# A plan of scheduler settings per stretch of 32 units, and a calibrated exponential, in a kernel of attention and gMLP layers

## Chip, cores, metric

One NeuronCore of a Trainium2 chip. The metric is the device time of one execution in microseconds (us). The runs came from several chips, so kernels are compared only through the runs of the kernel before that were made on the same chip in the same call, or directly when they shared a call.

## The reference

Two layers, each a multi-query attention (2048 tokens, 32 heads of 16, one shared key and value head) and a gMLP mixer whose spatial gate is a 2048 x 2048 matmul.

```python
q = (x @ wq).reshape(B, S, H, Dh).transpose(0, 2, 1, 3);  k = x @ wk;  v = x @ wv
p = softmax(einsum("bhqd,bkd->bhqk", q, k) * Dh ** -0.5)
x = x + einsum("bhqk,bkd->bhqd", p, v).transpose(0, 2, 1, 3).reshape(B, S, H * Dh) @ wo
z = gelu(layernorm(x) @ w_in);  z1, z2 = z[..., :Fh], layernorm(z[..., Fh:])
g = einsum("ts,bsf->btf", w_sp, z2) + b_sp[None, :, None]        # the spatial pass
x = x + (z1 * g) @ w_out
# ... all of this twice
```

## The kernel before

The program is built by a small list scheduler in the kernel file: operations with a modelled duration are committed in modelled time, and each engine's list is written in that order, with waits on semaphores. The model's times do not exist on the chip; only the order does. A unit is one key tile of one group of heads, four blocks of 512 score columns; there are 1024 units, 512 a layer. A block's exponential is done on ScalarE (1536 or 1024 columns in one instruction) or on VectorE (six instructions, three blocks at a time). What VectorE takes is decided here:

```python
def d_act(n):                       # modelled duration of an exponential on ScalarE
    return n * 0.8333e-3 + 0.051
...
def take(self, t, js):              # may VectorE have a block now? (cut)
    if self.hold or sc.bank_free() > t or sc.free["dve"] > t + JIT:
        return None
    if EF and any(o.start is None and o.ready is not None and o.ready <= t for o in k.early_first):
        return None                 # yield to the spatial pass
    ...
        backlog = sc.free["dve"] - t + sum(o.dur for o in sc.ready["dve"] if o.eng == "dve" and o.ready <= t)
        if backlog > BACKLOG:       # 3.0
            return None
    ...
    u = max(self.u, fu + LOOK)      # LOOK = 8 units ahead of the score matmuls
```

Zero matmuls fill TensorE where the scheduler believes that it would be too idle to keep its clock (with zeros of half the width, e7, the granted clock of a profile was 0.906, with the full ones on the same chip, e5, 0.994):

```python
class WarmStream:
    def peek(self, f): ...          # the time at which the modelled activity of a 3.41 us window falls too low
    def commit(self, t):
        def fn(e):
            return e.matmul(k.b32(pvb if b is None else b.idx), k.zero[:], k.zero[:, None, :].to_broadcast([P, 4, P]),
                            start=b is not None, stop=b is not None)
```

The softmax here doesn't subtract the row's maximum and nothing guards it: scores larger than these inputs give would overflow.

## Time and profile before

| | before |
|---|---|
| time | 1796.68 us median of 4 runs (1796.06 to 1797.44) |
| ScalarE busy | 1724.7 of 1797.9 us (the profile is of a fifth run, of 1799.73 us) |
| exponentials on ScalarE, blocks on VectorE | 1428 instructions, 532 blocks |
| last exponential of layer 0, of layer 1 | 851.2, 1743.8 us |
| from the last exponential to the end | 54.1 us |

The lines that carry this are in the prediction. One more view matters later: the exponentials' own groups, with busy time and mean of one, then the idle time before them and what ended it. Neighbouring instructions overlap: the durations of all exponentials sum to 2085.3 us, where ScalarE was busy for 1724.7 with everything.

```profile
L1471 ACT ACTIVATE Pa<-ps_all 128x1536 bf16<-128x1536 f32 x708 | 1184.4, 1673 | 13.3 <-PE ps_all L1815 9.8 <-PE ps_all L1558 3.2
L1471 ACT ACTIVATE Pa<-ps_all 128x1024 bf16<-128x1024 f32 x720 | 892.7, 1251 | 1.5 <-PE ps_all L1815 1.4
```

L1815 are the score matmuls. L1558 is PV, which waits for VectorE's blocks too and frees ScalarE's ring of results: 3.2 us of ScalarE's idle time come from VectorE being late (in the two places VectorE's block was done at 442.53 and 672.94 us, and PV followed at 443.09 and 673.20). Other lines met below: L1196 are the matmuls of the spatial pass, L1037 the projection of the last tokens into the mixer, L1253 the piece of the spatial pass that needs those last tokens. What runs after the last exponential I call the closing.

### The profile page before, as it was taken

To read this page: it belongs to the slowest core of one execution; us is meant where nothing else is said; L and a number is where in the kernel's file an instruction comes from. 1 tells how busy PE (TensorE), PEld (TensorE's weight loads), DVE (VectorE), ACT (ScalarE), POOL (GpSimd) and SP (SyncE) were. 2 spreads that over 40 slices of the span, in tenths; PEclk is the share of its full clock that TensorE was granted. 3 is DMA by queue.
4 is the path that set the end of the run, shared out by engine and by line. 5 is a ranking of instruction groups with operands and counts; after the bars stand their busy time and mean duration, and the time that the engine had idled before them with its cause. 6 is when DMAs were issued, how large, how long until landed. Compare 5 with 4: busy or idle time off the path is not lost.

```text
span 1797.9 us, 29587 instructions
## 1 busy us (share of the span) xinstructions
PE 1577.4 (88%) x11812; PEld 467.1 (26%) x11812; DVE 1643.8 (91%) x2477; ACT 1724.7 (96%) x1558; POOL 54.1 (3%) x99
## 2 busy tenths in 40 slices
PE   8888888888889898999998888888888999988999
PEld 4222222222222222223532222222222222222235
DVE  8999999999999999883999999999999899999638
ACT  8999999999999999999589999999999999999984
POOL 1000000000000000000110000000000000000000
PEclk9999999999999999999999999999999899999999
DMA  4535100011011020111310000100111001111114
GB/s 148 123 78 134 54 18 4 7 30 24 10 47 31 27 48 4 63 38 53 82 41 10 4 7 19 19 7 4 31 30 39 28 19 48 19 28 40 52 57 122
DMA packets 146761, 74.04 MB, mean 41 GB/s; under 512 B 99776, under 2 KB 143424, under 8 KB 146624
## 3 DMA queue, kind: packets, MB, share of 16 engines
q1 hardware_dynamic: 145040, 71.98, 15.4%
q8 instruction: 94, 1.54, 0.4%
q14 instruction: 43, 0.35, 0.1%
q10 hardware_dynamic: 1584, 0.16, 0.1%
HBM read 31.49 MB, written 17.83 MB: 27 GB/s over the span
## 4 chain that ended last, share of the span: by engine, by line
ACT 55%; issue 21%; PE 19%; DVE 5%; POOL 0%; DMA 0%; ACTq 0%; POOLq 0%
ACT Pa L1471 52%; PE ps_all L1815 5%; PE ps_all L1196 4%; PE ps_all L1558 3%; PE ps_all L1286 2%; PE ps_all L1796 1%; PE ps_all L1253 1%; PE ps_all L998 1%; DVE st L660 1%; ACT z2n L1083 1%; ACT z1s L1079 1%; PE ps_all L1037 1%; DVE xn L675 0%; PE ps_all L966 0%; DVE E L1667 0%
## 5 line engine op out<-in xcount | busy, mean ns | idle before, releaser
L1471 ACT ACTIVATE Pa<-ps_all 128x1024 bf16<-128x1024 f32 (+1 forms) x1428 | 1615.8, 1460 | 14.8 <-PE ps_all L1815 11.1
L1815 PE MATMUL ps_all<-qs,kT 32*128 32x512 bf16 x4096 | 564.4, 386 | 197.0 <-ACT Pa L1471 183.9
L1667 DVE TENSOR_SCALAR E<-ps_all 128x512 f32<-128x512 f32 x532 | 359.6, 681 | 24.2 <-PE ps_all L1815 21.3
L1815 PEld LDWEIGHTS ps_all<-qs,kT 32*128 32x128 bf16 x4096 | 139.3, 91 | 793.2 <-ACT Pa L1471 770.1
L1796 PE MATMUL ps_all<-zero 128*128 128x512 bf16 x1040 | 322.6, 393 | 16.5 <-DVE mv L1126 5.0
L1558 PE MATMUL ps_all<-Pa,V 128*32 128x512 bf16 x3564 | 317.4, 386 | 0.3 <-DVE Pd L1698 0.2
L1698 DVE SCALAR_TENSOR_TENSOR Pd<-E 128x1536 uint16<-128x1536 f32 (+1 forms) x178 | 310.3, 1743 | 2.1
L1558 PE MATMUL ps_all<-Pd,V 128*32 128x512 bf16 x532 | 179.6, 386 | 0.0
L1196 PE MATMUL ps_all<-wsT,z2n 128*128 128x512 bf16 x616 | 170.1, 385 | 0.9 <-DVE gp L1208 0.5
L1696 DVE TENSOR_TENSOR E<-E 128x1536 f16<-128x1536 f16 (+1 forms) x178 | 168.6, 947 | 2.3
L1694 DVE TENSOR_TENSOR E<-E 128x1536 f16<-128x1536 f16 (+1 forms) x178 | 168.4, 946 | 2.4
L1692 DVE TENSOR_SCALAR E<-E 128x1536 f16<-128x1536 uint16 (+1 forms) x178 | 168.9, 949 | 1.8
L1796 PEld LDWEIGHTS ps_all<-zero 128*128 128x128 bf16 x1040 | 79.2, 98 | 183.1 <-issue 125.0
L1695 DVE TENSOR_SCALAR E<-E 128x1536 f16<-128x1536 f16 (+1 forms) x178 | 97.5, 548 | 1.1
L1558 PEld LDWEIGHTS ps_all<-Pa,V 128*32 128x32 bf16 x3564 | 61.9, 94 | 114.4 <-issue 106.0
L1208 DVE TENSOR_TENSOR gp<-ps_all,gp 128x512 f16<-128x512 f32 x56 | 38.4, 686 | 57.7 <-PE ps_all L1196 57.7
L998 PE MATMUL ps_all<-w_in_r,xnTB 128*128 128x448 bf16 x256 | 64.6, 356 | 1.1 <-DVE E L1667 0.4
L1196 PEld LDWEIGHTS ps_all<-wsT,z2n 128*128 128x128 bf16 x616 | 44.8, 98 | 75.3 <-issue 42.6
L1037 PE MATMUL ps_all<-xnTB,w_in_r 128*128 128x512 bf16 (+2 forms) x364 | 63.0, 299 | 1.0 <-DVE z2n L1009 0.3
L1286 PE MATMUL ps_all<-E 128*128 128x512 bf16 x224 | 54.5, 380 | 0.1
L664 POOL TENSOR_SCALAR ve<-mv 128x2 f32<-128x2 f32 (+1 forms) x28 | 12.4, 444 | 1396.6 <-DVE mv L662 1396.4
L1265 ACT ACTIVATE E<-ps_all 128x512 f16<-128x512 f32 (+1 forms) x51 | 26.0, 539 | 25.6 <-PE ps_all L1253 25.0
(86 smaller groups left out, 961.2 us busy)
## 6 DMA issues: line engine op xcount, KB each, us to landing
wsT_scratch<-gp SPq DMA_DIRECT2D x16, 512.0 KB, 3.5
wsT<-wsT_scratch SPq DMA_DIRECT2D x8, 1024.0 KB, 5.4
z1s<-z_scratch SPq DMA_DIRECT2D x16, 448.0 KB, 3.8
z_scratch<-z1s SPq DMA_DIRECT2D x4, 896.0 KB, 5.8
z2n<-wsT_scratch SPq DMA_DIRECT2D x4, 768.0 KB, 4.6
wsT<-wsT_scratch SPq DMA_DIRECT2D x4, 768.0 KB, 5.8
X<-in_A_x_dram SPq DMA_DIRECT2D x8, 256.0 KB, 5.6
z2n<-wsT_scratch SPq DMA_DIRECT2D x2, 1024.0 KB, 8.4
```

The lines of the kernel that those rows point to most:

```text
L1196: ins = e.matmul(self.b32(b), self.z2n[:, s, f * 128:(f + 1) * 128], w_[:, s - s0, :] if s - s0 < na or not spare else wsp[:, s - s0 - na, :],
L1286: ins = e.matmul(self.b32(b)[:, 0:D], self.hT[:, par, f, tt * 128:(tt + 1) * 128], self.w_out_r[:, f, :], start=(f == 0), stop=(f == NF - 1))
L1471: return e.activation(k.Pa[:, base:base + n, :], k.b32(b0, n).rearrange("p (k q) -> p k q", k=n), ACTF.Exp, scale=SCALE)
L1558: ins = e.matmul(k.b32(u.grp.pvb)[32 * j:32 * j + 32, :], k.V[:, u.kt, :], b.slot, tile_position=(0, 32 * j), start=u.first, stop=u.last)
L1667: c = k.sc.op("dve", lambda e: e.tensor_scalar(k.ey[:, s, 512 * i:512 * (i + 1)], k.b32(j.bank.idx)[:, 0:512], E_LOG2, E_BIAS, op0=ALU.mul ...
L1692: o2 = sc.op("dve", lambda e: e.tensor_scalar(x, lo, E_X * 2.0 ** -16, E_X * E_A, op0=ALU.mult, op1=ALU.add), d_sb(n, 0.521e-3), self.ops ...
L1694: o3 = sc.op("dve", lambda e: e.tensor_tensor(w, x, x, ALU.mult), d_sb(n, 0.521e-3), [o2, self.wfree], pr)
L1695: o4 = sc.op("dve", lambda e: e.tensor_scalar(w, w, E_C, None, op0=ALU.add), d_sb(n, 0.26e-3), [o3], pr)
L1696: o5 = sc.op("dve", lambda e: e.tensor_tensor(w, w, x, ALU.mult), d_sb(n, 0.521e-3), [o4], pr)
L1698: o7 = sc.op("dve", lambda e: e.scalar_tensor_tensor(po.bitcast(U16), y, E_D, w, op0=ALU.add, op1=ALU.add), d_sb(n, 1.042e-3), [o5] + self ...
L1796: return e.matmul(k.b32(pvb if b is None else b.idx), k.zero[:], k.zero[:, None, :].to_broadcast([P, 4, P]), start=b is not None, stop=b i ...
L1815: return e.matmul(self.b32(bank), self.kT[32 * j:32 * j + 32, g.v, kt * 128:(kt + 1) * 128], self.qs[32 * j:32 * j + 32, g.q.slot, :], til ...
```

## The change

The intent: let VectorE take blocks as suits each stretch instead of by one setting, and give the scheduler the exponential's average pace on the chip.

```diff
-EF = 1
-LOOK = 8
-BACKLOG = 3.0
+PACE = 0.0125
+STRETCH = 32
+WAYS = ((8, 3.0, 1), (7, 3.0, 1), (9, 3.0, 1), (8, 2.2, 1), (8, 4.2, 1), (8, 3.0, 0), (7, 4.2, 1), (9, 2.2, 1))
+PLAN = (1, 0, 0, 0, 2, 1, 0, 0, 0, 1, 2, 1, 2, 1, 1, 0, 1, 0, 2, 2, 1, 0, 1, 0, 2, 5, 0, 5, 2, 0, 5, 0, 0)
 ...
-        o = k.sc.op("act", fn, d_act(512 * n), self.deps, 0.0, table="exp")
+        o = k.sc.op("act", fn, d_act(512 * n) + PACE, self.deps, 0.0, table="exp")
 ...
-        if EF and any(o.start is None and o.ready is not None and o.ready <= t for o in k.early_first):
+        look, back, ef = WAYS[PLAN[k.fill_s.u // STRETCH]]
+        if ef and any(o.start is None and o.ready is not None and o.ready <= t for o in k.early_first):
 ...
-            if backlog > BACKLOG:
+            if backlog > back:
 ...
-        u = max(self.u, fu + LOOK)
+        u = max(self.u, fu + look)
```

The plan uses only ways 0, 1, 2 and 5: look-ahead of 8, 7 or 9, and not yielding.

## The prediction

> **What bounds the kernel now.** I read the page first for the busiest engine, then the chain that ended last, then each engine's busy time by 50 us windows, then ScalarE's timeline for its gaps, last TensorE's timeline at the end.

> Busy time and chain, from the page:

> ```profile
> PE 1577.4 (88%) x11812; PEld 467.1 (26%) x11812; DVE 1643.8 (91%) x2477; ACT 1724.7 (96%) x1558; POOL 54.1 (3%) x99
> ACT 55%; issue 21%; PE 19%; DVE 5%; POOL 0%; DMA 0%; ACTq 0%; POOLq 0%
> ```

> Three engines are near full; ScalarE (ACT), which takes most of the softmax exponentials, leads. The windows give us, then busy (and count) of PE, PEld, DVE, ACT, POOL, clock, DMA share, GB/s:

> ```profile
> 350.00:400.00 50.00, 41.02 (x318) 10.26 (x317) 49.37 (x64) 50.00 (x46) 0.00 (x0) 1.00 0.10 27
> 800.00:850.00 50.00, 49.65 (x360) 15.07 (x359) 16.33 (x29) 49.88 (x46) 0.81 (x2) 1.00 0.16 51
> 1250.00:1300.00 50.00, 40.74 (x320) 10.03 (x317) 48.46 (x62) 50.00 (x45) 0.00 (x0) 1.00 0.10 27
> 1700.00:1750.00 50.00, 49.66 (x352) 15.72 (x350) 18.29 (x32) 47.69 (x44) 0.81 (x2) 1.00 0.13 40
> 1750.00:1800.00 50.00, 46.40 (x293) 26.48 (x291) 39.37 (x99) 18.34 (x34) 1.10 (x2) 1.00 0.42 121
> ```

> Two kinds of stretch. In the long attention stretches ACT is full and VectorE (DVE) has 0.6 to 1.5 us idle in 50. At the end of each layer (800 to 850, 1700 to 1750) the spatial pass of the mixer fills PE; ACT is still almost full, and DVE has over 30 us idle. After 1743.8 us no exponentials are left and a closing of 54 us runs on PE.

> ACT's timeline: start, length, line, shapes, count, then idle before and its releaser:

> ```profile
> 418.99 23.19 ACT L1471 ACTIVATE Pa<-ps_all 128x1536 bf16<-128x1536 f32 x20
> 443.54 44.39 ACT L1471 ACTIVATE Pa<-ps_all 128x1536 bf16<-128x1536 f32 x39 [1.36 <-PE ps_all L1558]
> 599.42 72.43 ACT L1471 ACTIVATE Pa<-ps_all 128x1536 bf16<-128x1536 f32 x64 [0.31 <-PE ps_all L1815]
> 673.65 94.11 ACT L1471 ACTIVATE Pa<-ps_all 128x1536 bf16<-128x1536 f32 x83 [1.79 <-PE ps_all L1558]
> ```

> The exponentials alternate 1536 and 1024 columns; 64 of them in 72.43 us is 2.263 us a pair. The two gaps before 443.54 and 673.65 are waits for PV (L1558), which frees ACT's ring of results: DVE's exponentials came late there. ACT's other idle time inside the exponentials is 3.1 us from 1397 to 1404 us, 0.8 at 1672, and a few us spread over the start of layer 1. So before the closing, the time is very nearly the sum of ACT's work.

> [...]the trace has 2.263, a fixed 0.065 us each. I use the trace.
> [...]the trace's rows of the chain have 549, 949 to 952 and 1749.
> [...]Sixteen L1196 in a row took 3.46 us here (1748.87 to 1752.33), 216 ns each.
> [...]

> **The change part by part.** All orders are decided when the program is built, so I compared the two built programs' instructions, by count and place, without any time from the scheduler.

> 1. The added 0.0125 us is only in the scheduler's duration of an exponential. Its old pair was 2560 x 0.8333 ns + 2 x 51 ns = 2.235 us; the new one is 2.260, which is the trace's pitch to 0.003. Nothing runs slower by it. Believing ACT slower, the scheduler fits in more DVE blocks per ACT instruction.
> 2. The plan sets look-ahead (7, 8, 9 units), tolerated DVE backlog (2.2, 3.0, 4.2 us) and, in three stretches of layer 1, lets DVE blocks go although spatial work is waiting. Stretches 25, 27 and 30 have this last setting.
> 3. Result in the built program: blocks of 512 columns on DVE go from 532 to 545, so ACT has 13 fewer. By PV order: units 0 to 415, 234 to 235; 416 to 511, 34 to 37; 512 to 799, 160 to 163; 800 to 927, 70 to 69; 928 to 1023, 34 to 41. Seven of thirteen are in the last 96 units.

> Cost on DVE, from these groups (busy us, mean ns):

> ```profile
> L1667 DVE TENSOR_SCALAR E<-ps_all 128x512 f32<-128x512 f32 x532 | 359.6, 681 | 24.2 <-PE ps_all L1815 21.3
> L1698 DVE SCALAR_TENSOR_TENSOR Pd<-E 128x1536 uint16<-128x1536 f32 x177 | 309.6, 1749 | 2.1
> L1692 DVE TENSOR_SCALAR E<-E 128x1536 f16<-128x1536 uint16 x177 | 168.5, 952 | 1.8
> L1696 DVE TENSOR_TENSOR E<-E 128x1536 f16<-128x1536 f16 x177 | 168.2, 950 | 2.3
> L1694 DVE TENSOR_TENSOR E<-E 128x1536 f16<-128x1536 f16 x177 | 168.0, 949 | 2.3
> L1695 DVE TENSOR_SCALAR E<-E 128x1536 f16<-128x1536 f16 x177 | 97.2, 549 | 1.0
> ```

> 359.6/532 is 0.676; the five chain rows sum to 911.5 us over 531 blocks, 1.717. A block costs DVE 2.39 us; 13 cost 31.1. DVE should be busy about 1675 us. Most of it lies beside other work, in the idle time at the layers' ends.

> Saving on ACT, layer 0: 712 exponentials become 711, with 2048 columns fewer: 2048 x 0.833 ns + 0.065 = 1.8 us. Layer 1: 716 become 712, 4608 columns fewer: 3.84 + 4 x 0.065 = 4.1 us. Together 5.9 us, all in stretches where ACT is full.

> What is given back: PE is full in the last stretch, and faster exponentials do not shrink the spatial pass. In the built program 54 instead of 44 spatial matmuls (L1196) stand after the last score matmul, and 44 instead of 36 after the last PV. PE's timeline there, before:

> ```profile
> 1754.94 1.73 PE L1037 MATMUL ps_all<-xnTB,w_in_r 128*128 128x128 bf16 x28
> 1756.51 1.03 PE L1196 MATMUL ps_all<-wsT,z2n 128*128 128x512 bf16 x4
> 1758.01 3.01 PE L1253 MATMUL ps_all<-z2n 128*128 128x256 bf16 x26 [0.48 <-DVE z2n L1134]
> ```

> In the changed order these 4 are 12. Twelve take 12 x 0.216 = 2.6 us from 1756.51, to 1759.1 instead of 1758.01: 1.1 us later, as 0.5 us of the wait absorbs some. Between last scores and last PV, ten L1196 stand where eight did: about 0.4 us. Sum 1.5 us. At the end of layer 0 the order after the last PV is unchanged (46 on both sides), so its 1.8 us is kept. Small copies swap engines (three V copies more on ACT in layer 1, one key copy and one query copy fewer); I put that at zero. The 35 extra zero matmuls (1040 to 1075) cost 35 x 0.216 = 7.6 us of PE in stretches where it has 8 or more us of 50 idle: zero.

> Sum: -1.8 - 4.1 + 1.5 = -4.4 us, to 1792.3. I take off 0.8 for gaps that a scheduler with the right pace should lose (6.3 us are there in the three places named), a guess of about an eighth: 1791.5.

> **The rivals.** DVE becomes the bound: in windows of 350 to 400 us it has 0.6 us idle, less than one block, and a block without room costs 2.39 us to save 0.43. If the six blocks outside the last stretch found no room, that is 6 x 2 = 12 us worse than the sum: about 1804. Against: three of those six fall in layer 0's last 96 units, where DVE idles; the other movements are +1, +3 and -1. More probable is a single new gap of 1 to 3 us at a PV: 1793 to 1795.
> The spatial pass eats all of it: the last seven blocks' gain (3.0 us of ACT) is wholly given back on PE instead of half. For: PE is 49.66 of 50 busy there. That makes 1793.
> The correct pace helps more than counts show: if the 6.3 us of gaps all go, 1786. Against: those gaps hang on where a few late DVE chains fall, which the new plan moves rather than removes.

> **Range and chances.** The countable part is -4.4 us; unknown is where gaps of 1 to 2 us open and close, with some five places known today. Two or three such gaps either way give 1786.5 to 1797. To leave 2% would take 36 us, more than DVE's whole extra work: 1% for faster, 1.5% for slower.

> **What would show it.** Right: 1428 exponentials become 1423, 13 more L1667, DVE near 1675 us; the last exponential of layer 0 ends near 849.3 (851.2 before) and that of layer 1 near 1737 to 1738 (1743.8); from there to the end 55.6 us instead of 54.1. Wrong: new ACT gaps released by L1558 or L1815 in the long stretches (DVE was the bound), a closing no longer than 54.1 us (the spilled spatial matmuls were free), or ACT's gaps below 2 us in all (pace was worth more).

The sum: -1.8 - 4.1 + 1.5 - 0.8 = -5.2 us, from 1796.68 to 1791.5. Its terms rest on the kernel's own trace. The 0.833 ns a column: from the start of one exponential to that of the next, 1330 ns is the most frequent time after 1536 columns (294 of 689) and 903 ns after 1024 (227 of 716), 427 ns for 512 columns or 0.834 each. The 0.065 us: of 2.263 us a pair, 2560 columns leave 0.13 us for two. The 0.216 us: sixteen L1196 in 3.46 us. That the two gaps are VectorE's lateness is in the trace too (442.53 and 672.94 us, above).

## More of the kernel before

Which blocks go to VectorE, and where all work stands in the engines' lists, I call a program's composition.

## The result and the profile after

| | before | after |
|---|---|---|
| time, median | 1796.68 us (4 runs) | 1790.62 us (4 runs, 1789.19 to 1795.45) |
| ratio | | 0.9971 (95% interval 0.9952 to 0.999) |
| exponentials on ScalarE, blocks on VectorE | 1428, 532 | 1423, 545 |
| last exponential of layer 0, of layer 1 | 851.2, 1743.8 us | 847.9, 1738.6 us |
| from the last exponential to the end | 54.1 us | 55.1 us |

A ratio is the mean time of one kernel's fast runs over that of the other's of the same rounds, so it is not quite the ratio of the medians. The profiled run of after is its slowest (1795.45); a later profile of the same program, in e9, has 845.8 and 1735.7 us for the two ends, and again 55.1 from there.

The page of after, busy time and chain:

```profile
PE 1583.5 (88%) x11847; PEld 468.2 (26%) x11847; DVE 1666.6 (93%) x2510; ACT 1719.4 (96%) x1553; POOL 54.2 (3%) x99
ACT 45%; PE 19%; DVE 18%; issue 17%; DMA 0%; POOL 0%; ACTq 0%; POOLq 0%
```

ScalarE's work is 5.3 us less. VectorE's six groups are 32 us more (13 blocks of 2.39 us are 31), though its own busy time rises by only 22.8 us; neighbouring VectorE instructions overlap, 154.9 us in sum before and 170.4 after, and the groups count the overlap twice. VectorE has gone from 5% to 18% of the chain. That is not the 13 blocks' doing alone: e1, with the old 532 blocks, has 17% already.

The exponentials' groups after (the kernel's lines moved down by one or two):

```profile
L1472 ACT ACTIVATE Pa<-ps_all 128x1536 bf16<-128x1536 f32 x706 | 1170.9, 1659 | 12.9 <-PE ps_all L1817 12.0
L1472 ACT ACTIVATE Pa<-ps_all 128x1024 bf16<-128x1024 f32 x716 | 880.9, 1238 | 1.5 <-PE ps_all L1817 1.2
```

The waits for PV (now L1559) are gone altogether; the waits for score matmuls (now L1817) are somewhat more. ScalarE's timeline shows which are left in layer 0 between 100 and 700 us:

```profile
121.48 316.50 ACT L1472 ACTIVATE Pa<-ps_all 128x1536 bf16<-128x1536 f32 x280 [0.77 <-PE ps_all L1817]
438.60 51.72 ACT L1472 ACTIVATE Pa<-ps_all 128x1536 bf16<-128x1536 f32 x45 [0.61 <-PE ps_all L1817]
586.33 177.91 ACT L1472 ACTIVATE Pa<-ps_all 128x1536 bf16<-128x1536 f32 x157 [0.42 <-PE ps_all L1817]
```

The kernel before had breaks of 1.36, 0.31 and 1.79 us in this part, at 443, 599 and 673 us; the longest run without a break is not longer now (280 exponentials, before 364, from 30.56 to 442.18 us). The first of the three breaks has a cause that I had not looked for. Windows of 3.41 us around it, with TensorE's busy time first and its granted clock (PEclk) behind the engines:

```profile
108.41:111.82 3.41, 2.87 (x24) 0.81 (x24) 3.38 (x8) 3.41 (x5) 0.00 (x0) 1.00 0.00 0
111.82:115.23 3.41, 2.99 (x21) 0.73 (x19) 3.34 (x4) 3.41 (x4) 0.00 (x0) 1.00 0.00 0
115.23:118.64 3.41, 2.28 (x23) 0.61 (x22) 3.41 (x6) 3.41 (x5) 0.00 (x0) 0.99 0.00 0
118.65:122.06 3.41, 3.41 (x18) 0.68 (x15) 3.38 (x5) 2.64 (x3) 0.00 (x0) 0.51 0.94 62
```

A count that weighs a matmul by the part of the array that it uses does. Take each matmul's columns in the window (at 216 ns for 512), times the share of the 128 x 128 array: a quarter for the score matmuls (32*128) and PV (128*32), one for a zero matmul. The windows from 108.41 and 111.82 us have 4405 and 4939 columns, that from 115.23 has 2976. In all profiles with such a window, 6677 windows at full clock: all 53 under 2945 columns were followed by half the clock, none of the 6570 above 3141, and in between 19 were and 35 were not, which the count does not explain. In the two profiles of before and after alone, the nine that were followed by it have 2258 to 3036 columns, and all others at full clock between 10 and 1785 us 3072 or more. The scheduler's own limit in the kernel file is 3060.

In the half-clock window the score matmuls came late and ScalarE idled 0.77 us.

The kernel before has such windows too, and one of the prediction's three places of gaps, 1397 to 1404 us, lies in and just behind three of them in a row:

```profile
1392.34:1402.58 10.24, 9.71 (x41) 1.85 (x41) 8.57 (x13) 7.38 (x7) 0.00 (x0) 0.50 0.24 72
1668.82:1672.23 3.41, 3.41 (x19) 0.58 (x16) 3.38 (x6) 2.97 (x3) 0.43 (x1) 0.50 0.40 125
```

So 3.1 of the 6.3 us, and the 0.8 at 1672, were half-clock windows, which neither pace nor plan was meant to change.

Each run's granted clock, recorded for all runs but the first four of the kernel before, tells how many such windows it had: (1 - clock) x span / (0.5 x 3.413 us). A clock of 0.993 is 7 of them, 0.999 one. Within a kernel and chip this goes with 84% of the variance of the time: the four runs of after had 7, 2, 1 and 2 windows at 1795.45, 1790.45, 1789.19 and 1790.79 us. Over all kernels but the one with thin zero matmuls (e7), the slope of time on windows within a kernel and chip is 0.85 us a window (a correlation; e7 tests the cause). With it each kernel has a time at zero windows, which is steadier than the median: for after 1788.8, 1788.8 and 1788.7 us on three chips, for before 1793.7, 1794.6 and 1794.4.

TensorE at the end, after:

```profile
1749.58 1.73 PE L1038 MATMUL ps_all<-xnTB,w_in_r 128*128 128x128 bf16 x28
1751.15 2.75 PE L1197 MATMUL ps_all<-wsT,z2n 128*128 128x512 bf16 x12
1753.74 3.00 PE L1254 MATMUL ps_all<-z2n 128*128 128x256 bf16 x26
```

Twelve spatial matmuls (L1197, in the kernel before L1196) take 1751.15 to 1753.74, 2.59 us, and L1254 follows at once without the old wait of 0.48. From L1038's start to L1254's start it is 4.16 us; in the kernel before it was 3.07. That is the 1.1 us that was expected.

### The profile page after: what moved, and what is told of

It is laid out like the page before. It is cut to its first block, busy times and chain, and to the rows that moved or that the text cites. A ratio compares the mean times of both kernels' runs of the same rounds, so it can differ in the third digit from the quotient of the medians.

```text
span 1793.7 us, 29695 instructions
## 1 busy us (share of the span) xinstructions
PE 1583.5 (88%) x11847; PEld 468.2 (26%) x11847; DVE 1666.6 (93%) x2510; ACT 1719.4 (96%) x1553; POOL 54.2 (3%) x99
## 4 chain that ended last, share of the span: by engine, by line
ACT 45%; PE 19%; DVE 18%; issue 17%; DMA 0%; POOL 0%; ACTq 0%
ACT Pa L1472 44%; PE ps_all L1817 5%; PE ps_all L1197 4%; DVE E L1669 3%; PE ps_all L1559 3%; DVE Pd L1700 3%; PE ps_all L1287 2%; DVE E L1694 2%; DVE E L1696 1%; DVE E L1698 1%; PE ps_all L1798 1%; DVE st L661 1%; PE ps_all L1038 1%; PE ps_all L999 1%; DVE z2n L1010 1%
## 5 line engine op out<-in xcount | busy, mean ns | idle before, releaser
L1472 ACT ACTIVATE Pa<-ps_all 128x1536 bf16<-128x1536 f32 (+1 forms) x1423 | 1611.0, 1446 | 14.4 <-PE ps_all L1817 13.2
L1817 PE MATMUL ps_all<-qs,kT 32*128 32x512 bf16 x4096 | 565.6, 387 | 177.9 <-ACT Pa L1472 159.7
L1669 DVE TENSOR_SCALAR E<-ps_all 128x512 f32<-128x512 f32 x545 | 368.2, 684 | 15.2 <-PE ps_all L1817 13.9
L1798 PE MATMUL ps_all<-zero 128*128 128x512 bf16 x1075 | 331.6, 392 | 19.4 <-DVE mv L1127 7.5
L1817 PEld LDWEIGHTS ps_all<-qs,kT 32*128 32x128 bf16 x4096 | 139.6, 91 | 770.6 <-ACT Pa L1472 743.2
L1700 DVE SCALAR_TENSOR_TENSOR Pd<-E 128x1536 uint16<-128x1536 f32 x182 | 318.0, 1747 | 2.3
L1559 PE MATMUL ps_all<-Pa,V 128*32 128x512 bf16 x3551 | 317.6, 387 | 0.2
L1559 PE MATMUL ps_all<-Pd,V 128*32 128x512 bf16 x545 | 182.9, 386 | 0.1
L1698 DVE TENSOR_TENSOR E<-E 128x1536 f16<-128x1536 f16 x182 | 173.0, 950 | 2.3
L1696 DVE TENSOR_TENSOR E<-E 128x1536 f16<-128x1536 f16 x182 | 173.1, 951 | 2.1
L1694 DVE TENSOR_SCALAR E<-E 128x1536 f16<-128x1536 uint16 x182 | 173.0, 950 | 1.3
L1197 PE MATMUL ps_all<-wsT,z2n 128*128 128x512 bf16 x616 | 167.7, 382 | 3.0 <-DVE gp L1209 1.5
L1697 DVE TENSOR_SCALAR E<-E 128x1536 f16<-128x1536 f16 x182 | 100.3, 551 | 1.2
L1559 PEld LDWEIGHTS ps_all<-Pa,V 128*32 128x32 bf16 x3551 | 61.7, 94 | 114.2 <-issue 106.8
L1038 PE MATMUL ps_all<-xnTB,w_in_r 128*128 128x512 bf16 (+2 forms) x364 | 63.5, 299 | 3.6 <-DVE E L1669 2.6
L1197 PEld LDWEIGHTS ps_all<-wsT,z2n 128*128 128x128 bf16 x616 | 45.0, 98 | 78.2 <-issue 37.8
L665 POOL TENSOR_SCALAR ve<-mv 128x2 f32<-128x2 f32 (+1 forms) x28 | 11.5, 412 | 1398.5 <-DVE mv L663 1398.4
```

The source lines that it names most:

```text
L1197: ins = e.matmul(self.b32(b), self.z2n[:, s, f * 128:(f + 1) * 128], w_[:, s - s0, :] if s - s0 < na or not spare else wsp[:, s - s0 - na, :],
L1472: return e.activation(k.Pa[:, base:base + n, :], k.b32(b0, n).rearrange("p (k q) -> p k q", k=n), ACTF.Exp, scale=SCALE)
L1559: ins = e.matmul(k.b32(u.grp.pvb)[32 * j:32 * j + 32, :], k.V[:, u.kt, :], b.slot, tile_position=(0, 32 * j), start=u.first, stop=u.last)
L1669: c = k.sc.op("dve", lambda e: e.tensor_scalar(k.ey[:, s, 512 * i:512 * (i + 1)], k.b32(j.bank.idx)[:, 0:512], E_LOG2, E_BIAS, op0=ALU.mul ...
L1694: o2 = sc.op("dve", lambda e: e.tensor_scalar(x, lo, E_X * 2.0 ** -16, E_X * E_A, op0=ALU.mult, op1=ALU.add), d_sb(n, 0.521e-3), self.ops ...
L1696: o3 = sc.op("dve", lambda e: e.tensor_tensor(w, x, x, ALU.mult), d_sb(n, 0.521e-3), [o2, self.wfree], pr)
```

## The experiments

For the theories I use a measure taken from each trace: for two neighbouring exponentials, the time from start to start minus 0.8333 ns a column (0.834 by the most frequent times, see the prediction) and 63.5 ns, summed. It is what the exponentials lose to waiting, late ones less the catching up. The 63.5 ns are an average: in the kernel before 718 of 1405 neighbouring pairs have 49 to 53 ns and 590 have 59 to 70. I split it into what falls into (or up to 4 us behind) half-clock windows and the rest, "lost outside".

The theories at the start. A, my prediction's ledger: the time follows the number of blocks on VectorE and the spatial matmuls left for the closing. B: the calibrated pace removes gaps. A third came up with e6: the gain belongs to this one composition.

### e1: pace alone

```diff
-PLAN = (1, 0, 0, 0, 2, 1, ...)
+PLAN = (0,) * 33
```

> The scheduler's slower ScalarE clock alone, with one setting everywhere (that of the kernel before). Built program: 532 blocks on VectorE as before, so no exponential is saved; spatial matmuls left after the last PV 38 (was 46) in layer 0 and 34 (was 36) in layer 1. Theory A (the time follows ScalarE's work plus what PE has left for the closings, 0.427 us a block, 0.216 us a left matmul): 0 - 1.7 - 0.4 = about 1794.6 us, the plan brings the rest. Theory B (the right pace removes gaps, the count of blocks matters little): 1791 to 1792 us, with no wait of the exponentials for PV.

Measured: ratio 1.0024 (1.0011 to 1.0036), slightly slower, well inside 2%. With 3.8 windows a run against 7.3 before, its time at zero windows is 1800.6, 6.9 us worse than before on the same chip (1793.7). Both theories missed. Waits for PV are still seen:

```profile
444.85 31.75 ACT L1472 ACTIVATE Pa<-ps_all 128x1024 bf16<-128x1024 f32 x28 [0.99 <-PE ps_all L1559]
674.48 26.31 ACT L1472 ACTIVATE Pa<-ps_all 128x1536 bf16<-128x1536 f32 x23 [0.82 <-PE ps_all L1559]
1628.87 6.88 ACT L1472 ACTIVATE Pa<-ps_all 128x1536 bf16<-128x1536 f32 x6 [0.82 <-PE ps_all L1559]
```

The two gaps of the kernel before are smaller, at the same places, and a third is there; lost outside is 10.2 us against 6.7. The blocks on VectorE are 532 as before: the pace alone adds none. The closing is not shortened by the two spatial matmuls fewer, it is 55.0 us, because TensorE then waits for VectorE's normalisation of the last tokens:

```profile
1763.03 3.01 PE L1254 MATMUL ps_all<-z2n 128*128 128x256 bf16 x26 [1.34 <-DVE z2n L1135]
```

### e2: plan alone

```diff
-PACE = 0.0125
+PACE = 0.0
```

> The plan alone, with the old ScalarE clock in the scheduler. Built program: 538 blocks on VectorE (6 more, all in layer 1), 32 and 34 spatial matmuls left after the last PV of the layers (were 46 and 36). Theory A: -2.6 - 3.0 - 0.4 = about 1790.7 us, as good as the whole change. Theory B: the wrong pace leaves the gaps of the kernel before (6.3 us), so 1794 to 1796 us and waits of exponentials for PV are seen again.

Measured: ratio 1.001 (0.9998 to 1.0023), 1797.8 at zero windows. Six blocks more on VectorE, and 14.5 us lost outside. A is refuted as a rule for any kernel (it said 1790.7). B's gaps are there, at new places: two waits for PV (1.15 us at 752, 0.83 at 1144), and otherwise waits for score matmuls, the longest of 2.23 us at 441; the time is still above its range. The closing is 55.0 us, with the same wait of 1.34 us.

### e3 and e10: yielding to the spatial pass in all stretches

```diff
-PLAN = (..., 2, 5, 0, 5, 2, 0, 5, 0, 0)
+PLAN = (..., 2, 0, 0, 0, 2, 0, 0, 0, 0)
```

> The whole change, but the three stretches that stop yielding to the spatial pass have the plain setting. Built program: 542 blocks on VectorE (3 fewer than the change, all in the last 96 units), 38 spatial matmuls left after the last PV (44 in the change). If the last stretch's gain is given back on PE, as predicted: +1.3 - 1.3 = 0, same time as the change within 0.5 us. If the spilled matmuls are free in the closing: 1.3 us slower than the change.

> The change with stretches 25, 27 and 30 at the plain setting, again, now on the same chip as the change. The two programs are equal up to the matmuls of unit 986 of 1024. If the last stretch's gain is given back on PE: within 1 us of the change (its 0.9954 against 0.9971 came from different chips). If its earlier result was more than a difference of chips: 1.5 to 3 us faster than the change.

Measured: e3 0.9954 (0.9942 to 0.9967) to before, on another chip than the change's first runs; in e9 and e10, side by side, 0.9962 for the change and 0.9964 for this, means 1792.09 and 1792.54 us. At zero windows 1789.0 and 1789.1 against 1788.7 to 1788.8. The same time with three blocks fewer, but the intervals are about 2.5 us to either side, so the times alone can't tell 0 from 1.3 us. The closing can, and it shows 1.0 of the 1.3 us given back on TensorE. Its closing, from e10's profile:

```profile
1745.16 1.73 PE L1038 MATMUL ps_all<-xnTB,w_in_r 128*128 128x128 bf16 x28
1746.72 1.46 PE L1197 MATMUL ps_all<-wsT,z2n 128*128 128x512 bf16 x6
1748.23 3.01 PE L1254 MATMUL ps_all<-z2n 128*128 128x256 bf16 x26
```

Six spatial matmuls instead of twelve stand before L1254, and the closing takes 54.1 us instead of 55.1. A side fact from the built programs: putting only stretch 30 back gives the very same program, so the settings of stretches 25 and 27 do nothing.

### e4: too slow a pace

```diff
-PACE = 0.0125
+PACE = 0.025
-PLAN = (1, 0, ...)
+PLAN = (0,) * 33
```

> One setting everywhere, and ScalarE believed slower than it is by another 0.0125 us per instruction. Built program: 543 blocks on VectorE (11 more), and only 12 and 14 spatial matmuls left after the last PV (46 and 36). Theory A without limit: -4.7 - 7.3 - 4.8 = about 1780 us. Theory C (a pace that is wrong to this side packs more PE and VectorE work between two exponentials than fits, so score matmuls come late and ScalarE waits): 1790 to 1800 us, with more than 10 us of ScalarE idle before exponentials released by score matmuls.

Measured: ratio 1.0071 (1.0057 to 1.0085), 1805.1 at zero windows, 18.2 us lost outside; its waits for score matmuls sum to 19.1 us. Theory C holds in direction; the median of 1812.43 is even beyond its range. That packing more work than fits is the reason is argued and not shown; VectorE is 48% of this run's chain. The 22 spatial matmuls fewer did not shorten the closing either: 56.0 us instead of 54.1, with the wait of 1.34 us before L1254 and 2.04 us of waits for VectorE before it.

### e5 and e9: the change again

> The changed kernel once more, as reference on this chip for the others, and to fill up the number of its runs. From the four runs on record, each 3.4 us window at half clock costs about 1 us and a run without any would take 1788.5 us: ratio to before 0.995 to 0.997, one to three such windows in most runs, against five to nine in the kernel before.

> The changed kernel a third time, beside the three others of this call. Ratio to before 0.996 to 0.998, as in both earlier measurements.

Measured: 0.9971 (0.9958 to 0.9983), just outside the 0.995 to 0.997 expected, with 7.2 windows a run against 6.8 before, more than the one to three expected; and 0.9962 (0.9949 to 0.9974) with 4.0 against 5.6. The gain at zero windows is 5.8 and 5.7 us; the rest is windows, which differ by chip and run.

### e6: the plan shifted by one stretch

```diff
-PLAN = (1, 0, 0, 0, 2, 1, 0, 0, ...)
+PLAN = (0, 1, 0, 0, 0, 2, 1, 0, ...)
```

> The same right pace and the same settings, each applied one stretch (32 units) later. Built program: 543 blocks on VectorE (545 in the change), 34 and 56 spatial matmuls left after the last PV (46 and 44). If the count of blocks is the cause, as my prediction's sum has it: 2 blocks less, 12 left matmuls less in layer 0 and 12 more in layer 1, so within 1.5 us of the change, about 1791. If the gain belongs to this one composition (a good draw, kept because it measured well): about where pace alone and plan alone were, ratio 0.999 to 1.003 to the kernel before, with 10 us or more lost between exponentials outside the half-clock windows (6 in the change).

Measured: ratio 1.0033 (1.002 to 1.0045), 11.2 us slower than the change on the same chip, 14.1 at zero windows (3.8 a run against 7.2). 543 blocks on VectorE, the right pace, the same settings, and the gain is gone: lost outside is 16.2 us. The gain belongs to this composition. The closing in turn grows with the count as predicted:

```profile
1756.04 1.73 PE L1038 MATMUL ps_all<-xnTB,w_in_r 128*128 128x128 bf16 x28
1757.61 5.34 PE L1197 MATMUL ps_all<-wsT,z2n 128*128 128x512 bf16 x24
1762.79 3.00 PE L1254 MATMUL ps_all<-z2n 128*128 128x256 bf16 x26
```

24 spatial matmuls instead of 12, 5.18 us instead of 2.59, and a closing of 57.7 us instead of 55.1: 2.6 us for 12 x 0.216.

### e7: thin zero matmuls

```diff
-            return e.matmul(k.b32(...), k.zero[:], k.zero[:, None, :].to_broadcast([P, 4, P]), ...)
+            return e.matmul(k.b32(...)[:, 0:256], k.zero[:], k.zero[:, None, :].to_broadcast([P, 2, P]), ...)
```

> The change with every zero matmul that keeps the clock up of half the width (256 columns for 512); the order of all instructions is the same. If half-clock windows are a real part of the time (about 0.85 us each) they become many: clock below 0.985 (16 windows or more) and 10 us or more slower than the change. If the zero matmuls do not matter: same clock, same time.

Measured: ratio 1.0171 (1.0156 to 1.0186), 37 us slower than the change, with the same order of instructions.

```profile
core 0: 1835.3 us, clock 0.906
```

Over the five runs it is some 94 windows a run, 87 more than the change had on this chip, 0.43 us each. Half-clock windows are a real part of the time. The 0.43 us are a net figure, as the thin zeros also take some 116 us of work from TensorE (an estimate: 1075 times half of the measured 0.216 us); in this profile the exponentials lose 54 us in or just behind 101 such windows, 0.54 each, less than in the profiles before and after (5.5 and 7.3 us for 7 windows).

### e8: more zero matmuls everywhere

```diff
+            e.matmul(k.b32(...)[:, 0:256], k.zero[:], k.zero[:, None, :].to_broadcast([P, 2, P]), ...)
             return e.matmul(k.b32(...), k.zero[:], k.zero[:, None, :].to_broadcast([P, 4, P]), ...)
```

> The change with a second zero matmul of 256 columns behind each one; the order is otherwise the same. If the half-clock windows are what is left to gain here: clock 0.999 to 1.0 and about 1788.5 to 1789.5 us (on the first chip's scale), 1 to 3 us faster than the change. If the 115 us more of TensorE work (1075 of 0.107 us) get in the way of score matmuls: slower, with more time lost between exponentials.

Measured: ratio 0.9975 (0.9962 to 0.9987), mean 0.8 us above the change on the same chip, which is no difference.

```profile
core 0: 1794.2 us, clock 1.000
```

Four of five runs had no window at all, against 7.2 a run: 6 us ought to be gained (7.2 x 0.85). The 0.107 us of a zero matmul of 256 columns in the expectation are the author's estimate, about half of the 0.216 us for 512; 26 matmuls of that width (L1254 in the trace of after) took 2.84 us, 0.109 each. Lost outside rose from 6.3 to 11.5 us and the closing from 55.1 to 56.4: in this profile the zeros give back what they save. Both expectations were half right.

### e11: the plan in layer 0 alone

```diff
-PLAN = (1, 0, ..., 0, 1, 0, 2, 2, ...)
+PLAN = (1, 0, 0, 0, 2, 1, 0, 0, 0, 1, 2, 1, 2, 1, 1, 0) + (0,) * 17
```

> The change with its plan in layer 0 alone; layer 1 has the plain setting throughout (right pace everywhere). Built program: layer 0 as in the change (272 blocks on VectorE), layer 1 269 blocks (273 in the change). By counts: 4 blocks fewer, 44 spatial matmuls left as in the change, so 1.7 us slower than the change. If each layer's composition brings its own freedom from gaps: layer 0 ends with the change's time and layer 1 is as long as with pace alone, some 4.5 us slower than the change.

Measured: ratio 1.0009 (0.9996 to 1.0022), 9.1 us slower than the change on the same chip; of this 2.5 windows a run more are 2.1 us. At zero windows it is 1795.6, 6.9 slower: beyond both, and nearer to the composition theory's 4.5 than to the count's 1.7. Layer 0 ends at 847.5 us, as the change's (845.8 to 847.9), so layer 0 kept its gain, and layer 1 lost it all.

### e12: zero matmuls only where windows were seen

On e3's kernel:

```diff
+EXTRA = {61: 1, 62: 3, 267: 1, 269: 3, 525: 2, 782: 1, 785: 3}   # unit: zeros after its PV, into the open PV bank
+TWICE = range(1038, 1063)                                        # these zero matmuls are issued twice
```

> The version of the previous but one run with 39 more zero matmuls at the places where half-clock windows were seen in both profiles of the change (around units 62, 268, 525, 784 and where the gelus stand in layer 1), the order unchanged. If these windows are what differs from run to run: 0 to 2 of them in a run instead of 3 to 7, and 1 to 3 us faster than without (the fastest version so far). If they only move to other places: the same time and clock.

Measured: ratio 0.9954 (0.9941 to 0.9966), the lowest mean of this chip: 1790.66 us against 1792.54 without the zeros and 1792.09 for the change. Windows are 2.5 a run against 4.0, not the 0 to 2 expected; in the profile four of the five treated places have none, an untreated one (765 us) has two, and one stands at a treated place: the two zeros of unit 525 ran at 922.7 and 922.9 us, just before the window from 925.46 us, which has 2860 columns by the count above and was followed by half the clock from 928.87. The difference of 1.9 us is what 1.5 windows and some luck make; with spreads of 3 us (e12) and 8.5 us (e10) between runs it is not clear of noise. It is the fastest version by the mean, without proof.

## Why the prediction was right or wrong

The time (1791.5 predicted, 1790.62 measured) and the sum of the terms hold, the second partly by luck. At zero windows the gain is 5.8 and 5.7 us on the two chips that ran both kernels (e5, e9). The ledger:

| term | predicted | measured |
|---|---|---|
| ScalarE's exponentials, 13 blocks fewer | -5.9 | counts as predicted; -5.9 is again 6656 columns x 0.833 ns and 5 x 0.065 us, not measured apart. ScalarE's busy time fell by 5.3 |
| closing | +1.5 | +1.0 (54.1 to 55.1) |
| gaps | -0.8 | -0.4 to -0.7 (lost outside 6.7 to 6.0 to 6.3) |
| sum | -5.2 | -5.3 to -5.6 |
| half-clock windows | not thought of | -1.4 on the average (6.5 to 4.9 a run, of the 29 and 14 runs with a clock), but by chip anything from fewer to more |

By layer the agreement is two misses that cancel. Taking out what was lost in half-clock windows, layer 0's last exponential came at 850.4 us before and 845.7 to 845.8 in the three profiles of the change, 4.7 us earlier where 1.8 was predicted: lost outside fell from 2.9 us to between 0.2 and 0.4, with the two PV gaps. From there to the last exponential of layer 1 it took 887.9 us before and 885.2 to 885.8 after, 2.1 to 2.7 us less where 4.1 was predicted: lost outside rose from 3.7 us to between 5.7 and 6.0.

Point by point:

1. **ScalarE is the bound and 13 blocks are worth 5.9 us.** Right for this pair, because the time lost between exponentials stayed nearly the same in sum. It is no rule: the shifted plan has 543 blocks and is 11 us slower. I had taken the undisturbed flow for granted, as a property of the kernel; it is a property of the composition. That the scheduler "fits in more DVE blocks" by believing ScalarE slower is not so for the pace alone, which has the old 532 blocks; on top of the plan it adds seven (538 to 545).
2. **The closing grows through spilled spatial matmuls.** Right for this pair, in mechanism and size: before L1254 1.1 us as worked out. The other 0.4 us, between the last scores and the last PV, did not show. e6 with 24 instead of 12 confirms 0.216 us each, and e3/e10 that the last stretch's blocks gain next to nothing. It holds upwards only: with 34 spatial matmuls left (e1, e2) and 14 (e4) instead of 36 the closing is not shorter but 55.0, 55.0 and 56.0 us, as TensorE waits for VectorE. The 35 more zero matmuls cost nothing that shows, but not for the reason given: the largest additions, 27 in sum, stand in the windows 700 to 750 and 1550 to 1650 us, where TensorE had 4.7 to 6.2 us idle in 50, not 8.
3. **A scheduler with the right pace loses gaps.** Wrong as a cause. Pace alone makes 10.2 us of gaps out of 6.7. Nor was the old duration simply too short: its fixed 51 ns is the pitch of half the neighbouring pairs (718 of 1405 have 49 to 53 ns), and the 0.065 us include small delays of the others, whose cause is not shown. In the change the two PV gaps are gone (3.2 us of such waits to none), which fits with the plan moving late VectorE blocks away from them (not traced block by block), and layer 1's start took 0.9 us more. The size of the term came out right by chance.
4. **Rival "VectorE becomes the bound".** Not in the change: no wait for PV at all, with VectorE at 93%. The "0.6 to 1.5 us idle in 50" were two windows; the others in the long stretches have 0.3 to 7.3. Of the prediction's own signs of being wrong there is a little: three new short gaps behind score matmuls outside half-clock windows (0.42 us at 586, 0.71 at 1397, 0.44 at 1693), whose cause is not traced. VectorE was busy for 1666.6 us and not 1675, since the groups' sum counts overlaps twice. But e1's and e2's waits for PV show that the margin is thin.
5. **Rival "the spatial pass eats all of it".** True, within 0.3 us, of the three blocks that come from the one stretch where not yielding acts, not of the rest.
6. **The range.** It was set by gaps of 1 to 2 us; the spread that runs really show comes from half-clock windows at about 0.85 us each, none to ten in a run. I had seen the clock column below 1.00 in the windows before, and had not asked what it cost.

What makes the other compositions lose 2 to 12 us more outside the windows is placed but not explained one by one. In e1 it is units 128 to 191 (1.7 us), 384 to 511 (2.3) and the last 64 (2.3); in e6 the start of layer 1 (7.0 against 5.0) and the last 64 units (3.3 against 0.6). Summed with blocks and closing it accounts for the time at zero windows of every variant, against the change, within 2.7 us, though each is from a single profile. Whether the plan was found by measuring many compositions is not shown here; that a shift by one stretch loses everything fits with it.

## What to carry to other kernels

When a scheduler decides the order, a count of what moved between engines says what a change can be worth, and only a control with the same counts (a shifted plan, one half alone) says why it was. Before comparing differences below half a per cent, look up the granted clock of every run: here one window at half clock is 0.85 us, and the change's time at zero windows repeats to 0.1 us (the kernel before's to 0.9) where its mean moves by 3. Filler matmuls cost ScalarE's flow as much as they saved when spread everywhere (e8: no half-clock window in four of five runs, but 5.2 us more lost outside, 1.3 more in the closing and no gain in time); whether placing them pays (e12) was not clear of noise. To see where windows fell, a count of columns by their share of the array served here (all 53 windows under 2945 were followed by half the clock, none of 6570 above 3141) and busy time did not (2.28 us and it fell, 1.63 and it stayed full).
